# Forgetting attention with a GELU MLP on one core: the loads of batch 2's v issued by GpSimd, and two regroupings of matmuls

## The chip, the core and the metric

The kernel runs on one core of a Trainium2 chip. A core has a matrix engine (TensorE, "PE" in the profile; its weight loads are shown apart as "PEld"), a vector engine (VectorE, "DVE"), a scalar engine for activations (ScalarE, "ACT"), a general engine (GpSimd, "POOL") and an engine that mostly starts transfers (SyncE, "SP"). Transfers between main memory and the on-chip memory are moved by 16 DMA engines, whoever starts them. The engines run side by side, each through its own instructions in program order, and wait for one another by semaphores. Matmuls write to PSUM, a small memory of banks, from which VectorE or ScalarE must copy before a bank is used again.

The metric is the device time of one execution in microseconds (us).

## The reference

Eight batches of eight heads, 576 tokens, head width 64. Attention with a decay built from forget gates, causal, then a two-layer MLP with exact GELU over all 4608 tokens of width 512, inner width 2048:

```python
scores = scale * np.matmul(q, k.transpose(0, 1, 3, 2))
cum = np.cumsum(np.log(np.clip(f, 0.0001, 1.0)), axis=-1)
decay = cum[:, :, :, None] - cum[:, :, None, :]
scores = np.where(causal, -1000000000.0, scores + decay)
scores = scores - np.max(scores, axis=-1, keepdims=True)
attn = np.exp(scores)
attn = attn / (np.sum(attn, axis=-1, keepdims=True) + 1e-09)
x = np.matmul(attn, v)          # then (batch, token, head * 64)
...
h = x @ w_in
out = (0.5 * h * (1.0 + erf(h / sqrt(2)))) @ w_out
```

## The kernel before

**Stages of a batch.** The heads of a batch are worked in four pairs. For a pair, `scores` writes four tiles of scores (t = 0 to 3) to PSUM and ScalarE takes their exponentials (L312). Only what lies under the diagonal is computed, in the cuts of `STILES`. The diagonal blocks must be masked: for the pairs for which `on_pe` holds, PE adds a large negative number with further small matmuls (`after` and `key_of`) before the exponential; for all others GpSimd sets the masked places to zero afterwards (L314). `attend` (L333) multiplies the exponentials with the weighed v, `vw`, one head at a time, and `normalize` (L346, L347) divides by the sums, giving x. The decay is put into v: `weigh_v` (L271, GpSimd) multiplies v by weights per token. x is then transposed, by PE and a copy (`to_xT`, L366 and L369) in batches 0 and 1, by a transfer that SP starts (`x_dma`, L372) in the later ones. `gemm1` (L388) is the first GEMM: 16 blocks (`ffb`) of 128 inner columns, each of four matmuls, one per slice `kt` of 128 of the model width, that is, per head pair. After slice 3 ScalarE applies the Gelu (L408). Slice `kt` needs the transposed x of pair `kt`. The second GEMM of a batch is not a stage of its own: its matmuls are given out in steps, `take(fill, n)`, between the score and attention matmuls of the next batch, so that PE has work while ScalarE computes exponentials.

**The second GEMM of batch 0** is cut in three. `gemm2_first` (16 steps of one matmul, L520) runs in batch 1's attention with the first half of `w_out`, and its sums are kept in on-chip tiles `ot_of`, copied at L532. `gemm2_second` (L544) does the other half, the rows `kt` 8 to 15, in batch 2's attention: 8 steps into two banks of the pool `o`, then 8 steps into two banks of `m`. Each step is two matmuls of 64 rows. VectorE then adds both banks to `ot_of` (L552, then L504 in `sum_out`), which sets the banks free. `gemm2_rows` (L484) follows as the 17th step: by `PLAN_0` its first row of blocks takes the two `o` banks again.

**q and k.** GpSimd loads them a batch or more ahead (`load_qk_tokens`, L108). For batches from 2 on, SP transposes them by transfers (`transpose_dma`, L238: heads 0 to 3 of q, then of k, then heads 4 to 7 of each) into `tq` and `tk`, and VectorE sorts these into `qT` and `kT` (`untangle`, L252, eight copies for each pair). For batch 2 the `untangle` of its pairs 0 to 3 stands in VectorE's order beside the Gelu blocks 5, 8, 11 and 14 of batch 1, ahead of everything of batch 2's attention.

**v and w_out.** `load_v` loads v of a batch in five transfers (four of 256 KB and one of 128 KB), by SP unless told otherwise. There is a single buffer `v_sb`, free when the last `weigh_v` of the batch before is done. `w_out` comes in four quarters of 512 KB (`load_w_out`, L174, always GpSimd[...]); the quarters 2 and 3 hold the rows `kt` 8 to 11 and 12 to 15. They are issued in batch 1's attention after `behind` (L570), a small GpSimd copy that waits until k of batch 2 has landed.

**The order around the change.** It is written out by hand. In `second_attention` (batch 1), after the last scores, GpSimd has the gate and the two loads of `w_out`; SP has the four transposes of batch 2 (from 49.01 us) and, after the first blocks of the first GEMM, `load_v(2)`. GpSimd's next work after that are the copy of the tails (L378), `weigh_v(2, 0)` and `weigh_v(2, 1)`, then the loads of q and k of batch 3. In `attention` (batches 2 to 7) the first GEMM opens with five blocks whose slices are interleaved: the first two blocks in the two `m` banks, the next two in `o` banks (`spare()`), the fifth in a score tile (`more`). The other eleven follow one after the other.

Of the kernel before, what the change touches and what calls it, by code (L numbers as in the profile page):

```python
# [9 lines left out]
FP32 = mybir.dt.float32  # L10
# [5 lines left out]
P = 128  # L16
# [3 lines left out]
HP = 4  # L20
# [33 lines left out]
def kernel(  # L54
# [10 lines left out]
    nc = tc.nc  # L65
# [23 lines left out]
    s_psum = ctx.enter_context(tc.tile_pool(name="s_psum", bufs=2, space=PSUM))  # L89
# [25 lines left out]
    def load_v(b, h0=0, h1=H, eng=nc.sync, ns=range(NBLK)):  # L115
        if b >= B:
            return
        for n in ns:
            p0 = D if n == NBLK - 1 else 0
            eng.dma_start(  # L120
                v_sb[p0:P, h0:h1, n, :],
                v[b, h0:h1, K0[n] + p0 : K0[n] + P].rearrange("h p d -> p h d"),
            )
# [48 lines left out]
    def load_w_out(c):  # L172
        kt = slice(c * n_ff // 4, (c + 1) * n_ff // 4)
        nc.gpsimd.dma_start(w_out_sb[:, kt, :], w_out_r[:, kt, :])  # L174
# [105 lines left out]
    e_of = {}  # L280

    def scores(b, i, t):
        on_pe = b == 0 or (b == 1 and i == 0)
        st = s_psum.tile([P, 2, 512], FP32, tag="s", name=f"s{t}")
        c = 0
        for n, q0, w in STILES[t]:
            z = D if n == NBLK - 1 else 0
            masked = on_pe and c in SDIAG[t]
            for half in range(-1, 2 if masked else 0):
                if half == 0 and z:  # L290
                    continue
                for h in range(2):
                    d = slice(h * D, (h + 1) * D)
                    if half < 0:
                        to = st[:, h, c + z : c + w]
                        ab = kT[i][d, K0[n] : K0[n] + P], qT[i][d, q0 + z : q0 + w]
                    else:
                        last = (half + 1) * D
                        to = st[:, h, c + z : c + last]
                        c0 = (1 + h - half) * D  # L300
                        ab = key_of[d, c0 : c0 + P], after[d, c0 + z : c0 + last]
                    nc.tensor.matmul(  # L302
                        to, *ab, start=half < 0, stop=half == 1 or not masked
                    )
            c += w
        z = D if t == 1 else 0
        if z:
            et = e4[(b * HP + i) % len(e4)]
        else:
            et = e_pool.tile([P, 2, 512], BF16, tag=f"e{t}", name=f"e{t}")  # L310
        e_of[b, i, t] = et
        nc.scalar.activation(et[:, :, z:c], st[:, :, z:c], Act.Exp, scale=scale)  # L312
        for c0 in [] if on_pe else SDIAG[t]:
            nc.gpsimd.affine_select(  # L314
                out=et[:, :, c0 + z : c0 + P],
                in_=et[:, :, c0 + z : c0 + P],
                compare_op=Alu.is_ge,
                fill=0.0,
                base=z,
                pattern=[[0, 2], [1, P - z]],  # L320
                channel_multiplier=-1,
            )
# [31 lines left out]
    def xT(b):  # L354
        if b not in xT_of:
            xT_of[b] = xT_pool.tile([P, n_dm, XC], BF16, tag="xT", name="xT")
        return xT_of[b]
# [25 lines left out]
    def gemm1(c, ffb, kts=range(4), ps=None, act=True):  # L383
        src = xT(c) if c < B else tails
        if ps is None:
            ps = m_psum.tile([P, TC], FP32, tag="m", name="ps1")
        for kt in kts:
            nc.tensor.matmul(  # L388
                ps,
                w_in_sb[:, kt, ffb * P : (ffb + 1) * P],  # L390
                src[:, kt, 0:TC],
                start=(kt == 0),
                stop=(kt == n_dm - 1),
            )
        if n_dm - 1 in kts and act:
            gelu(c, ffb, ps)
        return ps

    def spare():
        return o_psum.tile([P, TC], FP32, tag="o", name="ps1")  # L400

    def gelu(c, ffb, ps):
        if c not in g_of:
            g_of[c] = [
                g_pool.tile([P, TC], BF16, tag=f"g{n}", name=f"g{n}")
                for n in range(n_ff)
            ]
        nc.scalar.activation(g_of[c][ffb], ps, Act.Gelu)  # L408
# [147 lines left out]
    def gemm2_third():  # L556
        yield from gemm2_second(0)
        yield from gemm2_rows(0, PLAN_0)
        yield from gemm2_rows(1, PLAN_1)

    def take(gen, n):
        for _ in range(n):
            if next(gen, "end") == "end":
                return


    def behind(t, h):

        g = x_pool.tile([P, 1], FP32, tag="gate", name="gate")
        nc.gpsimd.tensor_copy(g[:PT], t[:, h, 0:1])  # L570
# [109 lines left out]
    def attention(b):  # L680


        fill = gemm2_third() if b == 2 else gemm2_rows(b - 1, PLAN)
        counts = FILL_2 if b == 2 else FILL

        def av(i, n=0):
            for h in range(2):
                attend(b, i, h, (0, 1, 2, 3, 4))
                normalize(b, i, h)
                if h == 0:  # L690
                    take(fill, n)
            x_dma(b, i)

        for i in range(HP):
            for t in range(4):
                scores(b, i, t)
                take(fill, counts[i][t])
                if t == 1 and 0 < i < (HP if b == 2 else HP - 1):
                    av(i - 1)
                    if b == 2 and i == 1:  # L700
                        load_v(3)
                if b == 2 and (i, t) == (0, 3):
                    weigh_v(b, 2)
                    weigh_v(b, 3)
                if b > 2 and i == 0 and t == 1:
                    load_v(b + 1)
                if b > 2 and t == 0 and i < 2:
                    transpose_dma(b + 1, 4 * i, 4 * i + 4)
                if b == 2 and t == 1 and i == 1:
                    transpose_dma(3, 0, 4)  # L710
        if b == 2:
            take(fill, 4)
            av(HP - 1)
        else:
            av(HP - 2)
            take(fill, 3)
            av(HP - 1, 1)
            put_off.pop()()
        take(fill, 4)
        if b == 2:  # L720
            transpose_dma(3, 4, 8)
        take(fill, 999)

        pss = [gemm1(b, ffb, (0, 1)) for ffb in range(2)]
        for ffb in range(2):
            gemm1(b, ffb, (2,), pss[ffb])
        pss += [gemm1(b, ffb, (0, 1, 2), spare()) for ffb in (2, 3)]
        for ffb in range(4):
            gemm1(b, ffb, (3,), pss[ffb])
        more = s_psum.tile([P, 2, 512], FP32, tag="s", name="ps1")  # L730
        gemm1(b, 4, ps=more[:, 0, :])
        if b + 1 < B:
            untangle(b + 1, 0)
            weigh_v(b + 1, 0)
        x_tail(b)

    def second_attention():


        b, fill = 1, gemm2_first(0)  # L740

        def av(i, h):
            attend(b, i, h, (0, 1, 2, 3, 4))
            normalize(b, i, h)

        def transposes(i, pool, tag):
            for which in range(2):
                transposes_first(b, i, which, pool, tag)


        nc.scalar.activation(warm[0:1, 0:1], warm[0:1, 0:1], Act.Exp)
        def tiles(i, t):
            scores(b, i, t)
            scores(b, i, t + 1)

        def run(i):
            av(i, 0)
            av(i, 1)

        tiles(0, 0)  # L760
        transposes(1, o_psum, "o")
        transposes(2, m_psum, "m")
        transposes(3, o_psum, "o")
        tiles(0, 2)
        take(fill, 2)
        tiles(1, 0)
        run(0)
        tiles(1, 2)
        take(fill, 4)
        weigh_v(1, 2)  # L770
        tiles(2, 0)
        run(1)
        weigh_v(1, 3)
        tiles(2, 2)
        take(fill, 4)
        tiles(3, 0)
        transpose_dma(2, 0, 4)
        transpose_dma(2, 4, 8)
        to_xT(b, 0, nc.vector.tensor_copy, o_psum, "o")
        to_xT(b, 1, nc.vector.tensor_copy, o_psum, "o")  # L780
        take(fill, 2)
        tiles(3, 2)
        behind(qk_of[2][1], H - 1)
        load_w_out(2)
        load_w_out(3)
        run(2)
        take(fill, 4)
        av(3, 0)
        both = s_psum.tile([P, 2, 1024], BF16, tag="s", name="ps_x2")
        to_xT(b, 2, nc.scalar.copy, ps=both[:, 0, 0:XC])  # L790
        av(3, 1)
        gemm1_begin(1, both)
        x_tail(1)
        load_v(2)

    for b in range(B):
        if b == 0:
# [64 lines left out]
```

## Time and profile before

Five runs took 336.2 to 338.64 us, the median is 336.64. The profile is of one execution that took 336.2 us; its span, from the first to the last instruction, is 334.3 us.

| | us |
|---|---|
| median of five runs | 336.64 |
| profiled execution | 336.2 |
| its span | 334.3 |
| PE busy in 33 to 58 (batch 1's attention) | 22.99 of 25 |
| PE busy in 58 to 100 (batch 1's first GEMM, batch 2's attention) | 41.42 of 42 |
| PE busy in 100 to 288 | 185.57 of 188 |
| GpSimd stands before weighing v of batch 2 | 14.08 |

A row of the order by time reads: start, duration (both in us from the span's start), engine, line, operation, what it writes and what it reads, shapes, how many instructions were merged; in brackets the idle time of the engine before it and what ended it. An "issue" row on SP or POOL is the engine's time to start the transfer, not the transfer. The view of the transfers gives, for a stretch of time, each queue's packets, megabytes and the time that its packets took as a share of 16 engines; q0 is the queue of GpSimd's transfers, q1 that of SP's. Some matmul records are missing in a trace, so a count can be one or two short of what the program issues.

### The profile page before, as it was taken

How to read it: one execution, taken by the hardware profiler on the slowest of the kernel's cores; microseconds unless marked ns; L12 is line 12 of the kernel's file. 1: busy time of each engine (PE TensorE's matmuls, PEld its weight loads, DVE VectorE, ACT ScalarE, POOL GpSimd, SP SyncE). 2: the span in 40 equal slices, each digit the busy share in tenths (PEclk: the TensorE clock that was granted, in tenths of full speed). 3: DMA queues.
4: the chain of work that ended last, by engine and by line, in shares of the span. 5: the costliest groups of instructions: out<-in, count | busy, mean ns of one | idle time of the engine just before them, and what ended most of it. 6: DMA issues, size and time to landing. Idle time of an engine off the chain costs nothing.

```text
span 334.3 us, 7780 instructions
## 1 busy us (share of the span) xinstructions
PE 321.8 (96%) x3121; PEld 171.0 (51%) x3161; DVE 181.2 (54%) x420; ACT 206.6 (62%) x296; POOL 126.5 (38%) x252
## 2 busy tenths in 40 slices
PE   7899989999999999999999999999999999999995
PEld 3674556445554466445644565446544654444443
DVE  5770547664449845894589547954796550020011
ACT  3987797774635786478827892798278846404600
POOL 8880575047427054714444354525441420000000
PEclk9999999999999999999999999999999999999999
DMA  7999999969999799399938994869700241011013
GB/s 108 220 200 193 196 192 132 195 120 210 192 190 177 116 209 180 91 138 166 222 105 119 171 197 145 120 127 208 174 6 2 91 72 46 0 66 63 0 39 86
DMA packets 101747, 44.16 MB, mean 132 GB/s; under 512 B 80336, under 2 KB 96976, under 8 KB 101712
## 3 DMA queue, kind: packets, MB, share of 16 engines
q1 hardware_dynamic: 84112, 28.73, 43.7%
q0 software_dynamic: 17200, 14.42, 28.4%
q8 instruction: 24, 0.39, 0.5%
q10 hardware_dynamic: 400, 0.52, 0.4%
q14 instruction: 11, 0.09, 0.1%
HBM read 36.85 MB, written 9.44 MB: 138 GB/s over the span
## 4 chain that ended last, share of the span: by engine, by line
PE 90%; issue 2%; DMA 2%; POOL 2%; DVE 1%; ACT 1%; POOLq 0%; ACTq 0%; DVEq 0%
PE ps L388 36%; PE ps L484 26%; PE o L333 10%; PE ps L424 8%; PE s L302 7%; DMA v_sb<-in_v_dram 2%; PE ps L544 1%; PE ps_x L366 1%; ACT e L312 1%; POOL q L108 1%; POOL k L108 1%; DVE qT L219 0%; DVE kT L219 0%; PE ps L520 0%; PE ps_f L208 0%
## 5 line engine op out<-in xcount | busy, mean ns | idle before, releaser
L408 ACT ACTIVATE g<-ps 128x512 bf16<-128x512 f32 x144 | 82.1, 601 | 83.8 <-PE ps L388 83.8
L312 ACT ACTIVATE e<-s 128x896 bf16<-128x896 f32 (+2 forms) x128 | 100.0, 836 | 21.1 <-PE s L302 18.4
L388 PE MATMUL ps<-xT,w_in_sb 128*128 128x512 bf16 x497 | 111.8, 379 | 0.7
L484 PE MATMUL ps<-w_out_sb,g 64*128 64x512 bf16 (+1 forms) x692 | 104.4, 376 | 1.6 <-issue 1.3
L388 PEld LDWEIGHTS <-w_in_sb 128*128 128x128 bf16 x576 | 55.9, 98 | 67.8 <-issue 2.3
L314 POOL TENSOR_SCALAR_AFFINE_SELECT e<-e 128x256 bf16<-128x256 bf16 (+1 forms) x135 | 49.3, 386 | 89.4 <-ACT e L312 89.1
L484 PEld LDWEIGHTS <-g 64*128 64x128 bf16 (+1 forms) x711 | 39.4, 95 | 34.8 <-issue 4.2
L271 POOL TENSOR_TENSOR vw<-v_sb,wT 128x640 bf16<-128x640 f32 x30 | 38.6, 1289 | 27.1 <-PE ps L544 14.1
L302 PE MATMUL s<-qT,kT 64*128 64x320 bf16 (+4 forms) x384 | 43.4, 276 | 2.9 <-ACT e L312 2.1
L252 DVE COPY kT<-tk 64x288 bf16<-64x288 bf16 x96 | 41.9, 436 | 3.6 <-DMA tk<-k 2.0
L252 DVE COPY qT<-tq 64x288 bf16<-64x288 bf16 x96 | 40.8, 425 | 1.7 <-DMA tq<-q 0.3
L492 DVE COPY ot<-ps 128x512 f32<-128x512 f32 x20 | 13.8, 692 | 47.0 <-PE ps L484 47.0
L333 PEld LDWEIGHTS <-e 128*128 128x128 bf16 x960 | 34.5, 98 | 8.1 <-POOL e L314 2.5
L333 PE MATMUL o<-vw,e 128*128 128x65 bf16 x960 | 37.2, 194 | 0.9 <-issue 0.8
L347 DVE TENSOR_TENSOR x<-o,r 128x320 bf16<-128x320 f32 x64 | 31.4, 491 | 2.7 <-DMA xT<-x 0.6
L433 DVE COPY ot<-ps 128x512 f32<-128x512 f32 (+2 forms) x9 | 5.7, 632 | 49.7 <-PE ps L424 49.7
L302 PEld LDWEIGHTS <-kT 64*128 64x128 bf16 x384 | 19.7, 94 | 23.8 <-issue 6.9
L424 PE MATMUL ps<-w_out_sb,g 128*128 128x512 bf16 (+2 forms) x142 | 27.9, 355 | 0.1
L424 PEld LDWEIGHTS <-g 128*128 128x128 bf16 x144 | 13.5, 98 | 14.5
L346 DVE RECIPROCAL r<-o 128x5 f32<-128x5 f32 x64 | 12.0, 188 | 11.2 <-PE o L333 11.1
L504 DVE TENSOR_TENSOR ot<-ot,ps 128x512 f32<-128x512 f32 x22 | 15.1, 685 | 1.1
L388 PE MATMUL ps<-tails,w_in_sb 128*128 128x512 bf16 x63 | 14.2, 377 | 0.1
(68 smaller groups left out, 137.9 us busy)
## 6 DMA issues: line engine op xcount, KB each, us to landing
out_dram<-ot SPq DMA_DIRECT2D x32, 256.0 KB, 2.5
v_sb<-in_v_dram SPq DMA_DIRECT2D x24, 256.0 KB, 4.6
q<-in_q_dram POOLq DMA_DIRECT2D x6, 576.0 KB, 6.3
k<-in_k_dram POOLq DMA_DIRECT2D x6, 576.0 KB, 8.4
v_sb<-in_v_dram SPq DMA_DIRECT2D x17, 128.0 KB, 4.9
w_in_sb<-in_moe_w_in_dram POOLq DMA_DIRECT2D x4, 512.0 KB, 8.2
w_out_sb<-in_moe_w_out_dram POOLq DMA_DIRECT2D x4, 512.0 KB, 9.4
v_sb<-in_v_dram POOLq DMA_DIRECT2D x5, 128.0 KB, 6.0
```

The lines of the kernel that those rows point to most:

```text
L252: nc.vector.tensor_copy(rows[:, odd], src[odd * D : (odd + 1) * D, 2 * i + h].rearrange("d j p -> d p j"),)
L271: eng.tensor_tensor(vw(b)[:, hs, n0:n1, 0:D], v_sb[:, hs, n0:n1, :], w.unsqueeze(3).to_broadcast([P, 2, n1 - n0, D]), Alu.mult,)
L302: nc.tensor.matmul(to, *ab, start=half < 0, stop=half == 1 or not masked)
L312: nc.scalar.activation(et[:, :, z:c], st[:, :, z:c], Act.Exp, scale=scale)
L314: nc.gpsimd.affine_select(out=et[:, :, c0 + z : c0 + P], in_=et[:, :, c0 + z : c0 + P], compare_op=Alu.is_ge, fill=0.0, base=z, pattern=[[ ...
L333: nc.tensor.matmul(o[:, m, :], e_of[b, i, t][:, h, c : c + P], vw_of[b][:, 2 * i + h, n, :], start=(n == 0), stop=(n == m),)
L347: nc.vector.tensor_tensor(x_of[b, i][:, :, h, :], o[:, :, 0:D], r.unsqueeze(2).to_broadcast([P, NBLK, D]), Alu.mult,)
L388: nc.tensor.matmul(ps, w_in_sb[:, kt, ffb * P : (ffb + 1) * P], src[:, kt, 0:TC], start=(kt == 0), stop=(kt == n_dm - 1),)
L408: nc.scalar.activation(g_of[c][ffb], ps, Act.Gelu)
L424: nc.tensor.matmul(pss[ts][:, c0:c1], g_of[c][kt][:, ts * P : (ts + 1) * P], w_out_sb[:, kt, c0:c1], start=(kt == 0), stop=(kt == n_ff - 1),)
L484: nc.tensor.matmul(banks[r], g_of[c][kt][rows, ts * P : (ts + 1) * P], w_out_sb[rows, kt, :], start=kt == (steps.index("r") if r else 0), ...
L504: nc.vector.tensor_tensor(ot, ot, bank, Alu.add)
```

## The change

It has four edits.

1. The mask of pair 3's tile 3 in batch 1 is done by PE instead of GpSimd.
2. Two steps of `gemm2_first` are taken earlier: four instead of two after pair 0's scores, two instead of four before `av(3, 0)`. The number in all stays 16.
3. `load_v(2)` is issued by GpSimd, between the gate and the two last quarters of `w_out`, instead of by SP at the end of `second_attention`.
4. In `attention` the opening of the first GEMM takes slices 0 and 1 of four blocks, then their slice 2, then slices 0 to 2 of the fifth block, then slice 3 of all five. Before, slice 2 of the first two blocks came after four matmuls and the fifth block followed whole.

```diff
     def scores(b, i, t):
-        on_pe = b == 0 or (b == 1 and i == 0)
+        on_pe = b == 0 or (b == 1 and (i == 0 or (i, t) == (HP - 1, 3)))
...
         pss = [gemm1(b, ffb, (0, 1)) for ffb in range(2)]
-        for ffb in range(2):
+        pss += [gemm1(b, ffb, (0, 1), spare()) for ffb in (2, 3)]
+        for ffb in range(4):
             gemm1(b, ffb, (2,), pss[ffb])
-        pss += [gemm1(b, ffb, (0, 1, 2), spare()) for ffb in (2, 3)]
-        for ffb in range(4):
+        more = s_psum.tile([P, 2, 512], FP32, tag="s", name="ps1")
+        pss.append(gemm1(b, 4, (0, 1, 2), more[:, 0, :]))
+        for ffb in range(5):
             gemm1(b, ffb, (3,), pss[ffb])
-        more = s_psum.tile([P, 2, 512], FP32, tag="s", name="ps1")
-        gemm1(b, 4, ps=more[:, 0, :])
...
         tiles(0, 2)
-        take(fill, 2)
+        take(fill, 4)
         tiles(1, 0)
...
         behind(qk_of[2][1], H - 1)
+        load_v(2, eng=nc.gpsimd)
         load_w_out(2)
         load_w_out(3)
         run(2)
-        take(fill, 4)
+        take(fill, 2)
         av(3, 0)
...
         gemm1_begin(1, both)
         x_tail(1)
-        load_v(2)
```

## The prediction

> **What bounds the kernel now.** I read the page's busy shares first, then the chain of waits. The profiled execution took 336.2 us, its span is 334.3; the median of the runs, 336.64, is 0.44 above it.
>
> ```profile
> span 334.3 us, 7780 instructions
> ...
> PE 321.8 (96%) x3121; PEld 171.0 (51%) x3161; DVE 181.2 (54%) x420; ACT 206.6 (62%) x296; POOL 126.5 (38%) x252
> ```
>
> Both say TensorE; "POOL 38%" says nothing of when GpSimd's work is due. So a gain can only be a hole in PE that closes, and a loss is whatever makes PE stand. Busy time by stretch (33 to 58, 58 to 100, 100 to 288 us) gives PE 22.99 of 25.00, 41.42 of 42.00 and 185.57 of 188.00 us: what can be won is about 2 us in batch 1's attention, which the order by time shows to be rounds between PE and ScalarE:
>
> ```profile
> 42.30 0.37 PE L302 MATMUL s<-qT,kT 64*128 64x256 bf16 x4 [0.41 <-ACT e L312]
> 42.89 0.34 PE L302 MATMUL s<-qT,kT 64*128 64x64 bf16 x4 [0.23 <-ACT e L312]
> ```
>
> PE waits there until an exp has freed one of two score tiles.
>
> **Part 1, batch 1's attention.** Two steps of `gemm2_first` move ahead to 41.50, where two steps of 0.216 us stand before the 0.41 us hole. Four end at 41.50 + 0.86 = 42.36; with 0.10 for the change from whole-array matmuls to scores (a GEMM of 64 x 0.216 = 13.81 us takes 13.91 to the next score) the scores of pair 1 start at 42.46 instead of 42.30. Those 0.16 us pass through the exps and shrink, as every round has a 0.23 us hole; I carry 0.05 to the scores (3,3) at 51.22. These now take the mask on PE: masked scores took 41.17 to 41.50, unmasked ones 51.22 to 51.45, so +0.09. Pair 2's attention thus ends 0.14 later. Then two steps fewer (-0.43), and the mask that GpSimd had at 53.07 (408 ns) no longer holds `attend(3, 0)`, whose sixth matmul stood 0.10. PE would be 0.39 ahead, but the transposes of pair 2 (L366, 53.86) wait for VectorE's x, which comes 0.14 later, at 53.62: they start at 53.67. **Gain 0.19 us**. The ot copy of the moved steps comes earlier and nobody waits for it.
>
> **Part 2, the opening of the first GEMM in batches 2 to 7.** It moves slice 2 from position 4 to 8 and slice 3 from 12 to 15. From the first matmul to the next stage the six GEMMs take 13.91, 13.91, 14.01, 13.91, 13.91 and 13.95 us (the last without the 0.10): only two hold a stall, 0.10 and 0.14, because the transposed x landed late. Gain 0.24. Its price: block 5 reuses block 0's bank five matmuls (1.08 us) after block 0's last. The first Gelu starts 0.41 after that matmul (137.89 to 138.31) and takes 0.60, so 1.01: hidden, by 0.07; were that cover gone, 0.05 a batch. **Gain 0.2 us**.
>
> **Part 3, v of batch 2.** Removed from SP: five issues of 10.15 us in all, for which nobody waits (SP's next work is a store at 72.59). The loads end in the 14 us for which GpSimd stands before weighing:
>
> ```profile
> 53.54 1.57 POOL L174 DMA_DIRECT2D w_out_sb<-in_moe_w_out_dram  x2
> 55.02 2.37 SPq L238 DMA_TRANSPOSE tk<-k  x1
> 57.49 10.15 SPq L120 DMA_DIRECT2D v_sb<-in_v_dram  x5
> 71.20 1.28 POOL L271 TENSOR_TENSOR vw<-v_sb,wT 128x640 bf16<-128x640 f32 x1 [14.08 <-PE ps L544]
> ```
>
> (L544 is not what it waits for; the last v packet moves at 70.2.) That wait costs nothing today: vw of batch 2 is first read at 80.33. So removing it brings 0. What counts is what the loads now stand before. On GpSimd five issues of 0.63 to 0.79 us (its own rows for v at 8 to 13 us), 3.6 us, go ahead of the two w_out loads, from about 53.0 to 56.7; behind them also stands the copy of batch 1's tails (56.71), which nobody reads before 302 us. And in the transfers: today v lies on SP's queue *behind* the transposes of batch 2's q and k; now it lies *beside* them. VectorE waits for those already:
>
> ```profile
> 62.37 1.34 DVE L252 COPY qT<-tq 64x288 bf16<-64x288 bf16 x4 [0.27 <-DMA tq<-q]
> 65.75 1.35 DVE L252 COPY kT<-tk 64x288 bf16<-64x288 bf16 x4 [2.04 <-DMA tk<-k]
> 67.11 1.34 DVE L252 COPY qT<-tq 64x288 bf16<-64x288 bf16 x4
> 68.46 1.34 DVE L252 COPY kT<-tk 64x288 bf16<-64x288 bf16 x4
> 71.16 0.69 DVE L552 TENSOR_TENSOR ot<-ot,ps 128x512 f32<-128x512 f32 x1 [1.36 <-PE ps L544]
> 71.88 0.69 DVE L504 TENSOR_TENSOR ot<-ot,ps 128x512 f32<-128x512 f32 x1
> ```
>
> Behind the copy that waits for tk stand two more copies (2.7 us) and the two adds that free the o banks. PE's 17th filling step (`PLAN_0`, L484, 73.03) takes those banks. So PE starts that step at (start of the kT copy) + 4.05 + 1.41 + 0.05 = start + 5.51. Today that is 71.26 and PE comes at 73.03: the last transpose may be 1.77 us later than 65.75, and no more.
>
> How late will it be? The DMA view of three stretches, 57 to 63, 9 to 12 and 13 to 15 us (packets, MB, share of 16 engines):
>
> ```profile
> q0 software_dynamic: 921, 0.93, 91.6%
> q1 hardware_dynamic: 927, 0.23, 30.4%
> ...
> q0 software_dynamic: 452, 0.33, 72.2%
> q1 hardware_dynamic: 1252, 0.31, 53.2%
> ...
> q0 software_dynamic: 168, 0.45, 104.6%
> ```
>
> q0 is GpSimd's queue, q1 SP's. In the first, w_out (1 KB packets) and the transposes (256 B) share the engines packet for packet. In the second v on SP beside GpSimd's q and k had 2.8 packets for one. The third is v on GpSimd alone: 109 of its 168 packets are of 4 KB, 55 a us, 290 ns each on its engine. No row shows that beside transposes; its cost is bounded by these shares.
>
> Two rules of the Trainium skill's page "DMA: Bandwidth & Descriptors" are to be weighed. Its section "Issuing engines are not separate DMA queues" says that the issuer changes only the issue time, since all transfers run on the same engines. By it part 3 costs 0 and the sum is 336.2 - 0.4 = 335.8. The section "Queues, rings and completion order" says that an engine takes turns between its queues a whole packet at a time. By it a 256 B transpose packet waits for a 4 KB one each time, which speaks against the change. The row 57 to 63 agrees with the second, the row 9 to 12 doesn't; I work out both.
>
> *One for one.* Transposes still to move when v starts (first packet 1.7 after the issue, as w_out: 54.7): two of 1152 packets, 2304. First 1.6 us as slow as w_out's start (55.2 to 56.8: 251 packets of q1), to 56.3. Then v, 1.18 MB = 288 packets at 51 a us (290 ns and 25 for a transpose packet): 5.6 us, to 61.9, with 288 transposes. Then w_out, 1024 at 150 a us (921 in 6): 6.8 us, to 68.7, with 1024. Left: 2304 - 251 - 288 - 1024 = 741. Meanwhile v has landed (62.9), GpSimd weighs (3.0) and issues q and k of batch 3 at 66 instead of 73.95, so q0 never runs dry; beside such loads q1 moved 972 packets in 29 to 34 us, 194 a us: 3.8 us, to 72.5. VectorE started 1.0 after the last packet (64.7, 65.75): 73.5. PE's step: 79.0 instead of 73.03, **+6.0 us**, whatever part 1 won before, as the transfers set it.
>
> *Three for one beside v, one for one beside w_out.* v 288 at 44 a us: 6.5 us with 864 transposes, to 62.8; w_out to 69.6 with 1024; left 165, 0.9 us: copy at 71.5, step at 77.0, **+4.0**.
>
> I take the first, as the row with the same transposes on the same queues is the nearest. Sum: 336.2 + 6.0 - 0.2 (part 2) = 342.0, or **342.5** on the median. With the lower share 340.5; with slower starts or copies slowed by GpSimd's work (600 ns instead of 330 each at 136 us, so up to +3.2) 345.5.
>
> **Rivals.** *w_out late.* If the transposes keep three for one throughout, 1189 are left after v at 62.8; a round of one w_out packet (95 ns) and three of 25 takes 171 ns, so 281 a us: done at 67.0, copy at 68.0, and VectorE costs 0.5. But 630 packets of w_out are left then: 3.8 us, landed at 71.8. Its last quarter is needed at 69.23 + 4 x 0.216 = 70.1: PE stands 1.7 us in L544, together 338.1 on the median (336.64 + 1.7 - 0.2, rounded). For it: the row 9 to 12; against it: 57 to 63.
>
> *The loads are hidden; not slower.* GpSimd's transfer is the more compact (16 times fewer packets for the same bytes), all ends by 69, as the bytes are the same and the first of them start 0.5 us earlier. Then parts 1 and 2 remain: 336.2. It holds as long as the last transpose lands before 67.5. Against it: v ended at 70.2 with the same bytes, and now the transposes get the small share of a mix that lasts as long.
>
> *A real gain.* Over 1.7 us would need most of the holes of batch 1, of which the edit fills one; its best sum is 0.39 + 0.24.
>
> **Chances.** VectorE's stall 0.67, w_out late 0.13, hidden 0.15, a gain 0.05. About 0.5% (1.7 us) is what this kernel's measurement tells from no change. Slower: the first two, 0.80; same 0.15; faster 0.05. The range 337 to 345.5 leaves out the last two but for a little, and 0.02 at the top.
>
> **What would show it.** Right: the kT copies from tk start after 70 us with a long DMA wait; idle time of PE before a L484 step near 73 with VectorE's add (L504) as releaser; GpSimd's weighing at 63. Wrong: kT copies as today; PE idle at 69 to 71 in L544 (w_out); or the scores of batch 2 start later than 69.0, which would put the loss in part 1.

## The result and the profile after

| | before | after |
|---|---|---|
| median, us (runs) | 336.63 (48) | 339.93 (27) |
| lowest to highest, us | 335.88 to 339.89 | 336.61 to 344.71 |
| ratio of the times, 95% interval | | 1.0064 [1.0045, 1.0083] |
| profiled execution, us | 336.2 | 340.52 |
| its span, us | 334.3 | 338.6 |

The change makes the kernel slower, by 0.64%, which is 2.15 us (336.63 x 0.0064; 1.5 to 2.8 by the interval). The forecast was 5.9 us slower (342.5 against 336.64). The ratios, here and below, leave out executions more than 1.5% above a kernel's fastest (here eight, at 342.1 to 344.7 us, seven of them at a granted clock of 0.99), which the medians keep; the traces below show that a long stand of PE costs clock, so the true harm is rather above 0.64% than below. The lowest time lies within the range of before and the highest is 5 us above it: something in the changed kernel is decided anew in each execution.

The line of busy shares in the page of the changed kernel says little by itself: PE is busy for 2.6 us more in a span that is 4.3 longer.

```profile
PE 324.4 (96%) x3125; PEld 172.4 (51%) x3165; DVE 184.0 (54%) x420; ACT 205.8 (61%) x296; POOL 131.1 (39%) x256
```

So I cut the traces at points that both kernels have: the first scores of batch 1, the first scores of batch 2, the opening of batch 2's first GEMM, the end. All lengths are in us, from the order by time.

| kernel | batch 1's scores to batch 2's | batch 2's scores to its GEMM | its GEMM to the end |
|---|---|---|---|
| before | 31.25 | 31.45 | 233.79 |
| after | 31.12 | 33.66 | 233.68 |
| after, profiled again (e8) | 31.12 | 33.42 | 233.64 |

The first and the third stretch are shorter than before (the small gains of parts 1 and 2), the second is 2.0 to 2.2 longer. (The first profile of the changed kernel also came 2.3 us late to batch 1's scores, 40.11 instead of 37.78. Up to there the two programs are the same. Two other traces, e4 without v on GpSimd and e6 with it, are 1.0 us late at this point. The cause was not looked for, and I leave the delay out; the times of the first profile below are to be read 2.2 us earlier.)

What happens in the second stretch? First PE in the order by time, before and then after:

```profile
69.23 1.89 PE L544 MATMUL ps<-w_out_sb,g 64*128 64x512 bf16 x16
71.12 1.89 PE L544 MATMUL ps<-w_out_sb,g 64*128 64x512 bf16 x16
73.03 1.89 PE L484 MATMUL ps<-w_out_sb,g 64*128 64x512 bf16 x16
```

```profile
71.43 1.03 PE L544 MATMUL ps<-w_out_sb,g 64*128 64x512 bf16 x8
73.31 1.04 PE L544 MATMUL ps<-w_out_sb,g 64*128 64x512 bf16 x8 [0.85 <-DMA w_out_sb<-in_moe_w_out_dram]
...
76.73 0.37 PE L484 MATMUL ps<-w_out_sb,g 64*128 64x512 bf16 x1 [0.30 <-DVE ot L552]
77.45 1.88 PE L484 MATMUL ps<-w_out_sb,g 64*128 64x512 bf16 x15 [0.35 <-DVE ot L504]
```

There are two new waits. After four steps of `gemm2_second`, PE stands for the last quarter of `w_out` (0.85 us); and the 17th step, L484, waits for both of VectorE's adds, as the forecast had it, but for 0.30 and 0.35 us instead of six. Counted from batch 2's first scores, the last L544 comes 1.03 us later than before and the second L484 another 1.18: in the order of time, 1.0 us passes at `w_out` and 1.2 at VectorE. VectorE's rows and GpSimd's of the same trace show where the second comes from:

```profile
69.13 3.44 DVE L252 COPY kT<-tk 64x288 bf16<-64x288 bf16 x4 [2.77 <-DMA tk<-k]
72.58 1.77 DVE L252 COPY qT<-tq 64x288 bf16<-64x288 bf16 x4
74.36 1.60 DVE L252 COPY kT<-tk 64x288 bf16<-64x288 bf16 x4
75.99 0.69 DVE L552 TENSOR_TENSOR ot<-ot,ps 128x512 f32<-128x512 f32 x1
76.71 0.69 DVE L504 TENSOR_TENSOR ot<-ot,ps 128x512 f32<-128x512 f32 x1
```

```profile
55.32 4.27 POOL L120 DMA_DIRECT2D v_sb<-in_v_dram  x5
...
69.25 1.33 POOL L271 TENSOR_TENSOR vw<-v_sb,wT 128x640 bf16<-128x640 f32 x1 [7.51 <-DMA v_sb<-in_v_dram]
```

The kT copies, which waited for tk until 65.75 before, start at 66.9 on the clock of before (69.13 less 2.2), not at 73.5 as forecast. They then take 3.44 + 1.77 + 1.60 = 6.81 us for twelve instead of 4.03, while GpSimd weighs v beside them from 69.25 on. And v is there at 67.0 (69.25 less 2.2), not at 62.9. Both terms of the forecast are off, in opposite directions.

The two waits of PE are not parts of a sum. The first add (75.99) follows the copies without a pause, so it did not wait for PE. The copies start 1.2 us later than before and take 2.8 us longer; less the slack of 1.77, that is 2.2 us, the whole by which the stretch grew. With `w_out` in time PE would have stood as long, all of it at L484. The wait for `w_out` lies inside VectorE's delay. (This is worked out from the trace; no run took the wait for `w_out` away and left the copies late.)

### The profile page after: what moved, and what is told of

Its sections match the earlier page's. It is cut to its first block, busy times and chain, and to the rows that moved or that the text cites. A ratio compares the mean times of both kernels' runs of the same rounds, so it can differ in the third digit from the quotient of the medians.

```text
span 338.6 us, 7790 instructions
## 1 busy us (share of the span) xinstructions
PE 324.4 (96%) x3125; PEld 172.4 (51%) x3165; DVE 184.0 (54%) x420; ACT 205.8 (61%) x296; POOL 131.1 (39%) x256
## 4 chain that ended last, share of the span: by engine, by line
PE 75%; DMA 15%; POOL 3%; DVE 2%; issue 2%; SPq 1%; ACT 0%; POOLq 0%; ACTq 0%
PE ps L388 28%; PE ps L484 26%; PE ps L424 8%; PE o L333 7%; DMA v_sb<-in_v_dram 6%; PE s L302 5%; DMA tk<-k 3%; DMA k<-in_k_dram 3%; DMA w_in_sb<-in_moe_w_in_dram 3%; DVE kT L252 1%; SPq L238 1%; POOL q L108 1%; POOL vw L271 1%; POOL k L108 1%; DVE qT L252 1%
## 5 line engine op out<-in xcount | busy, mean ns | idle before, releaser
L408 ACT ACTIVATE g<-ps 128x512 bf16<-128x512 f32 x144 | 81.0, 603 | 84.7 <-PE ps L388 84.7
L484 PE MATMUL ps<-w_out_sb,g 64*128 64x512 bf16 (+1 forms) x692 | 104.8, 376 | 2.2 <-issue 1.3
L484 PEld LDWEIGHTS <-g 64*128 64x128 bf16 (+1 forms) x711 | 40.3, 95 | 35.5 <-issue 5.4
L252 DVE COPY kT<-tk 64x288 bf16<-64x288 bf16 x96 | 44.6, 464 | 4.3 <-DMA tk<-k 2.8
L302 PE MATMUL s<-qT,kT 64*128 64x320 bf16 (+4 forms) x384 | 44.4, 276 | 1.9 <-ACT e L312 1.0
L504 DVE TENSOR_TENSOR ot<-ot,ps 128x512 f32<-128x512 f32 x22 | 15.1, 685 | 1.1
```

Source lines behind the costliest of these rows:

```text
L252: nc.vector.tensor_copy(rows[:, odd], src[odd * D : (odd + 1) * D, 2 * i + h].rearrange("d j p -> d p j"),)
L302: nc.tensor.matmul(to, *ab, start=half < 0, stop=half == 1 or not masked)
L484: nc.tensor.matmul(banks[r], g_of[c][kt][rows, ts * P : (ts + 1) * P], w_out_sb[rows, kt, :], start=kt == (steps.index("r") if r else 0), ...
L504: nc.vector.tensor_tensor(ot, ot, bank, Alu.add)
```

## Experiments

### Which part carries the loss: e1, e2 and e4

e1 is the kernel before with the move of v alone, e2 the changed kernel with v given back to SP at its old place, e4 the new opening alone.

```diff
         behind(qk_of[2][1], H - 1)
+        load_v(2, eng=nc.gpsimd)      # e1: on the kernel before
         load_w_out(2)
...
         x_tail(1)
-        load_v(2)                     # e1
```

> Part 3 alone: the kernel before, with load_v(2) issued by GpSimd ahead of the last quarters of w_out. Theory A (the transfers): w_out's last quarter and the transposes of k land late, PE stands about 0.9 us at the first L544 steps and up to 1 us at the first L484 step near 73 us; 1.5 to 3.5 us slower than before, as the whole change. Theory B (the loss lies in part 1 or 2, in the mask on PE, the moved steps or the five Gelus in a row): no change, within 0.5 us. Theory C (my forecast, transposes one packet for one of v): 4 to 6 us slower, with the copy from tk starting after 71 us.

> Parts 1 and 2 without part 3: the changed kernel with load_v(2) given back to SP at the end of second_attention. Theory A: 0.2 to 0.4 us faster than before (the sum of my parts 1 and 2), no stall in L544 or in the first L484 step. Theory B: about 2 us slower than before.

> Part 2 alone: the kernel before with only the new opening of the first GEMM in batches 2 to 7. Theory A and my forecast: 0 to 0.25 us faster, the stalls of 0.10 and 0.14 us in two of the six openings gone. Theory B (five Gelus in a row hold block 5 back): each opening longer by 0.1 to 0.4 us, 0.6 to 2.4 us slower in all.

| | median, us | ratio to before |
|---|---|---|
| e1, part 3 alone | 339.23 | 1.004 [1.0019, 1.006] |
| e2, parts 1 and 2 | 336.52 | 1.0001 [0.9984, 1.0018] |
| e4, part 2 alone | 336.4 | 0.9998 [0.9981, 1.0015] |

Part 3 carries the loss. The other two are too small for the times, but the traces show them: the stretch from batch 1's scores to batch 2's is 31.24 in e1 and 31.25 in e4, which lack part 1, and 31.12 in e2, which has it. In e2's trace batch 2's attention takes 31.45 as before: no wait is left.

The profiled execution of e1 took 343.37 us, 4.1 above its median. In it PE stands 3.5 us for `w_out` in one piece and 0.3 in another, no add of VectorE is waited for, and the stretch is 6.7 longer. But VectorE is late there too:

```profile
73.12 1.34 DVE L252 COPY kT<-tk 64x288 bf16<-64x288 bf16 x4 [7.50 <-DMA tk<-k]
```

This is 0.4 us from the 73.5 of the forecast, and 5.5 us of lateness for L484 by its chain; PE does not wait for the adds only because `w_out` and the lower clock hold it longer (L484 starts at 79.84). The same two delays stand side by side, both larger than in the changed kernel's traces. How often an execution goes this way is not known: the longest ones of the changed kernel have no trace.

### Before or behind w_out: e3

Is it enough that `w_out` goes first? In e3 GpSimd issues v after the two quarters.

```diff
-        load_v(2, eng=nc.gpsimd)
         load_w_out(2)
         load_w_out(3)
+        load_v(2, eng=nc.gpsimd)
```

> The changed kernel with GpSimd's load_v(2) behind the two quarters of w_out instead of ahead of them. Theory A with the order on GpSimd's queue as the cause: w_out lands at about 64 us again, L544 does not stand; if the 4 KB packets of v leave the transposes their share (as the trace of the changed kernel suggests, with 300 to 570 transpose packets a us beside them) k's transposes land by 66 and the time is 0 to 0.4 us below before. Theory C (one packet for one): from 63 us on the transposes get 51 packets a us while v takes 5.6 us, the copy from tk starts at about 70 us and the kernel is 2 to 3 us slower than before.

The median is 346.09, ratio 1.0285 [1.0261, 1.031], the worst kernel of all, and 9.6 us slower where one packet for one had been expected to cost 2 to 3. PE and VectorE by time:

```profile
79.77 4.29 PE L484 MATMUL ps<-w_out_sb,g 64*128 64x512 bf16 x16 [6.68 <-DVE ot L552]
```

```profile
69.69 1.34 DVE L252 COPY qT<-tq 64x288 bf16<-64x288 bf16 x4 [6.97 <-DMA tq<-q]
72.24 3.00 DVE L252 COPY kT<-tk 64x288 bf16<-64x288 bf16 x4 [1.21 <-DMA tk<-k]
75.26 2.38 DVE L252 COPY qT<-tq 64x288 bf16<-64x288 bf16 x4
77.66 1.33 DVE L252 COPY kT<-tk 64x288 bf16<-64x288 bf16 x4
79.03 0.69 DVE L552 TENSOR_TENSOR ot<-ot,ps 128x512 f32<-128x512 f32 x1
```

Read them from the bottom: the add that PE waits for comes straight after the copies, the copies straight after the transfer of tk. This is the forecast's chain in full and alone, since `w_out` is in time: late transposes, late and slow copies, late adds, and PE standing 6.68 us at the step that was named. It is what the forecast expected of the other order. The transfers between 64 and 68 us show its share, packet for packet:

```profile
q0 software_dynamic: 257, 0.84, 95.5%
q1 hardware_dynamic: 256, 0.06, 11.0%
```

While v's 4 KB packets (0.84 MB in 257) move on GpSimd's queue, SP's queue gets one 256 B packet for each, 64 a us.

### Are late copies the link? e5 and e6

In both, the last two `untangle` of batch 2 are moved behind adds in VectorE's order (after scores (0, 2) and (1, 0) of batch 2), where late transposes can't hold the adds up: e5 on e3, e6 on the changed kernel.

```diff
+                if b == 2 and (i, t) in ((0, 2), (1, 0)):
+                    untangle(b, 2 + i)
...
-                if late == 0:
+                if late == 0 and (b > 1 or at < 2):
                     untangle(b + 1, at)
```

> As e3_v_behind (9.5 us slower than before, PE 7.0 us at the first L484 step), but VectorE sorts q and k of pairs 2 and 3 of batch 2 later: untangle(2, 2) after the scores (0, 2) and untangle(2, 3) after the scores (1, 0) of batch 2, behind the adds that free the o banks. Theory A2 (the late transposes reach PE only through VectorE's order): the stall goes, time 0 to 0.5 us below before, though k's transposes land as late as in e3_v_behind, near 72 us. Theory B2 (PE stands for the transfers themselves, or for vw or w_out): still more than 3 us slower than before.

> The changed kernel with the same later place of untangle(2, 2) and untangle(2, 3). What is left is w_out behind v on GpSimd's queue. Theory A2: the L484 step does not stand, but L544 still does, 0.5 to 3.5 us, so 0.5 to 3.5 us slower than before (up to the whole loss of the change). If w_out were never late and only VectorE's order counted: within 0.4 us of before.

e5: 344.11, ratio 1.0216 [1.0198, 1.0235]. e6: 343.52, ratio 1.0135 [1.0099, 1.0171]. In e5 the step at 73 us no longer waits; its last L544 and first L484 come as early as before. So the order on VectorE was the link in e3. But the cure costs nearly as much as it saves. VectorE and GpSimd in e5:

```profile
74.63 6.11 DVE L252 COPY qT<-tq 64x288 bf16<-64x288 bf16 x4
80.75 1.55 DVE L252 COPY kT<-tk 64x288 bf16<-64x288 bf16 x4
82.33 0.69 DVE L492 COPY ot<-ps 128x512 f32<-128x512 f32 x1
```

```profile
75.91 1.84 POOL L314 TENSOR_SCALAR_AFFINE_SELECT e<-e 128x256 bf16<-128x256 bf16 x5
77.72 1.27 POOL L271 TENSOR_TENSOR vw<-v_sb,wT 128x640 bf16<-128x640 f32 x1
79.11 1.27 POOL L271 TENSOR_TENSOR vw<-v_sb,wT 128x640 bf16<-128x640 f32 x1
```

Four copies take 6.11 us instead of 1.34, one of them 3593 ns, while GpSimd works with hardly a pause; then PE waits 2.12 and 2.45 us for VectorE further on. My expectation had left this collision out. In e6, PE's wait for `w_out` is still there (1.49 idle, the last L544 1.94 late), which no order on VectorE could remove, and the same collision adds a wait of 2.45 for VectorE at 87.21. So in the changed kernel the wait for `w_out` is a second thing beside VectorE, not its consequence, and about as long: taking VectorE's lateness away at this place left 1.94 us.

### The size of the load, and the change once more: e7 and e8

e7 lets GpSimd load the heads 0 to 3 ahead of `w_out` and SP the heads 4 to 7 at the old place. e8 is the changed kernel itself.

```diff
-        load_v(2, eng=nc.gpsimd)
+        load_v(2, 0, 4, nc.gpsimd)
...
         x_tail(1)
+        load_v(2, 4, 8)
```

> The changed kernel with only heads 0 to 3 of v issued by GpSimd ahead of w_out (0.59 MB instead of 1.18), heads 4 to 7 by SP at the end of second_attention as before. If the loss goes with the bytes ahead of w_out, w_out lands about 3 us earlier than in the changed kernel: L544 does not stand; the transposes of k lie beside 144 instead of 288 packets of v; loss of 0 to 1 us. If what counts is that GpSimd's queue holds v packets of 4 KB at all, about the loss of the changed kernel, 2 us.

> The changed kernel once more, beside the others. 1.5 to 3 us slower than before, with a wide spread of its runs; a second trace, to see whether L544 and the first L484 step stand in it again and by how much: 0.5 to 4 us and 0 to 1 us. The 2.2 us that its first trace lost before 36 us should not come again.

e7: 336.96, ratio 1.0004 [0.9987, 1.0022]; the stretch is 31.46, no wait is left, though the kT copy starts at 66.59, 0.84 later than before (the eight copies ahead of it took 5.21 us instead of 2.68 while GpSimd weighed v and issued loads): within the slack of 1.77. e8: 339.46, ratio 1.0123 [1.0078, 1.0167] from six executions, 4.1 us by the ratio where 1.5 to 3 had been expected. Its PE and VectorE:

```profile
71.76 1.04 PE L544 MATMUL ps<-w_out_sb,g 64*128 64x512 bf16 x8 [1.35 <-DMA w_out_sb<-in_moe_w_out_dram]
```

```profile
69.22 1.34 DVE L252 COPY kT<-tk 64x288 bf16<-64x288 bf16 x4 [4.62 <-DMA tk<-k]
70.57 1.34 DVE L252 COPY qT<-tq 64x288 bf16<-64x288 bf16 x4
71.92 1.55 DVE L252 COPY kT<-tk 64x288 bf16<-64x288 bf16 x4
73.50 0.69 DVE L552 TENSOR_TENSOR ot<-ot,ps 128x512 f32<-128x512 f32 x1
```

In the order of time 1.72 of the 1.97 us pass at `w_out` (the last L544 against before) and 0.25 at VectorE. But here too the add follows the copies without a pause. The copies start 3.5 us later than before and take 0.2 longer; less 1.77, that is the whole 2.0 us again. In both profiles of this kernel VectorE's chain ends last and the wait for `w_out` lies inside its delay. The transfers of e8 from 57.2 to 63.1 us, while v moved (packets, MB, share of 16 engines), show where the forecast's arithmetic broke:

```profile
q0 software_dynamic: 341, 1.13, 83.8%
q1 hardware_dynamic: 1210, 0.30, 27.9%
```

The transposes put through 1210 packets beside v's 288 of 4 KB, where the forecast had 251 in v's slow start and 288 beside it, 539 in all. In the first profile of the change they put through even 2262 (57.2 to 66 us). The queues don't go side by side but by turns of a us or two: from 59 to 61 us of e8 the two queues moved 79 and 1153. Only after v, beside `w_out`, do they go packet for packet: 449 and 444 from 65 to 68 us, and 449 in 3 us are the 150 a us that the forecast had put in.

### Why v's queue pauses, and v held back: e9 and e10

One guess for the pauses was that VectorE's copies hinder GpSimd in issuing v. In e9 a small copy of Gelu block 3 keeps VectorE from the copies until 59.8. In e10 GpSimd issues v only behind `w_out` and a gate on tk's last transfer.

```diff
+                if b == 1 and ffb == 5:                    # e9
+                    hold = x_pool.tile([P, 1], FP32, tag="hold", name="hold")
+                    nc.vector.tensor_copy(hold, g_of[1][3][:, 0:1])
```

```diff
-        load_v(2, eng=nc.gpsimd)                           # e10
         load_w_out(2)
         load_w_out(3)
+        g = x_pool.tile([P, 1], FP32, tag="gate", name="gate")
+        nc.gpsimd.tensor_copy(g[:PT], tq_of[2][1][:PT, H - 1, JT // 2 - 1, 0:1])
+        load_v(2, eng=nc.gpsimd)
```

> The changed kernel, but VectorE's copies of q and k of batch 2 (untangle) begin only after the Gelu of block 3, at about 59.8 us, when GpSimd has issued all its loads. In the traces of the changed kernel GpSimd's queue runs dry for 1 to 2 us after v's first transfer while VectorE copies, and in that time the transposes of q pass alone. Theory D (VectorE's copies hold back GpSimd's writing of transfers): v's five issues take about 0.75 us each instead of 0.9, v moves without a pause at about 50 packets a us and has landed by 63.5, w_out's last quarter lands about 1 to 2 us earlier, and the transposes share one packet for one, so that k's land after 71 us. PE then stands at the first L484 step for 3 us or more, as I forecast, and the time is 3 to 8 us above before. Rival: the pause has another cause; then v moves with the same pause and q's transposes pass in it at 500 or more packets a us.

> The changed kernel with GpSimd's load_v(2) behind the two quarters of w_out and behind a small GpSimd copy that waits until k's last transpose has landed, so that v lies beside no transpose. If the loss comes from v lying beside the transposes and ahead of w_out: no stall at L544 nor at the first L484 step, v landed at about 72 to 73 us as in the kernel before, 0 to 0.4 us below before. If v on GpSimd's queue costs by itself (issue time, VectorE, its landing): more than 0.5 us above before.

The guess falls. e9 took 342.06, ratio 1.0153 [1.013, 1.0177]; GpSimd's issues took as long as in e8 (0.70 to 0.95 us each). VectorE stood idle from 56.7 to 59.8, and within that time, from 57 to 58 us, v's queue had a pause all the same:

```profile
59.81 0.15 DVE L824 CAST hold<-g 128x1 f32<-128x1 bf16 x1 [3.15 <-ACT g L408]
...
q1 hardware_dynamic: 477, 0.12, 98.7%
q0 software_dynamic: 4, 0.01, 3.5%
```

PE stands for `w_out` twice in it, 2.01 and 1.50 us. Why v's queue lets the transposes pass is left open.

e10 took 337.95, ratio 1.0047 [1.0025, 1.0069]. No matmul waits for `w_out` any more, and its stretch is 0.97 longer, not 2.0. What is left is GpSimd's issuing beside VectorE's copies, which its order by time shows:

```profile
66.39 1.94 DVE L252 COPY kT<-tk 64x288 bf16<-64x288 bf16 x4
68.35 2.17 DVE L252 COPY qT<-tq 64x288 bf16<-64x288 bf16 x4
```

GpSimd issues v from 66.35 to 70.93. Four copies take 1.94 and 2.17 us instead of 1.34, and the second L484 starts 0.32 late. The rest, 0.65, passes in the first attention matmuls of batch 2, where PE waits for a mask (0.21 idle at 81.64): GpSimd comes to the masks later, as it weighs v from 75.87. I had expected it to be no slower than before, and was wrong. Its trace also has two slow openings of the first GEMM (15.55 and 14.2 us instead of 13.91) where a transposed x landed late; whether v's place causes these I did not test (e1 and e2 each have one opening of 14.2 and 14.13). No version that puts all of v on GpSimd's queue was as fast as before, and none of the ten kernels was measurably faster than it.

## Why the prediction was wrong, step by step

- **What bounds the kernel.** Right: TensorE, and the loss is PE standing in batch 2's attention, where the slack was counted. It is the only stretch that grew. Both signs that the forecast had named came in the first profile: PE idle before L484 with L504 as the releaser (right), and PE idle in L544 for `w_out` (wrong).
- **Part 1, gain 0.19.** Right in sign, a little smaller: 31.25 to 31.12, 0.13 us.
- **Part 2, gain 0.2.** Right in the openings, and too small for the times. The six openings are 13.91 but for the last, 13.81; 14.01 and 13.95 have become 13.91 and 13.81. The stretch that holds them is shorter by 0.11 (after) and 0.15 (e8). No Gelu stall came: the cover of 0.07 held.
- **The wait of 14.08 us costs nothing.** Right: v is usable earlier than the 71.20 of before (67.0 in after, 64.54 in e8) and nothing is gained by it.
- **One for one, with v at 51 packets a us from 56.3 on.** This is the step that failed: a term of the sum, not the chain. It took the share of the row 57 to 63 us for a stretch in which v's queue came in bursts with pauses. The issues took 4.28 us, not 3.6, and v's first packet moved at 57.2 in e8, not at 54.7; what the transposes had left then was nearly as forecast (2366 packets from 57.2 to 68.7 us in e8, 2304 forecast). But 1210 of them moved beside v in e8 and 2262 in after, not 539. So the copies that wait for the last of them started 3.5 us later than before in e8 (69.22) and 1.2 in after, not 7.75 (73.5). After the slack of 1.77, and with copies slower by 0.2 and 2.8 us, which the forecast had only in its upper limit, VectorE's chain is late by 2.0 and 2.2 us, where 6.0 was forecast. That is the whole lengthening.
- **`w_out` beside it.** v was usable at 64.54 in e8, not 62.9, and `w_out` at 71.76, not 69.7. It holds PE up by 1.7 (e8) and 1.0 us (after), within the time that VectorE takes anyway.
- **The rivals.** "w_out late" named a wait that came. It gave 68.0 for the copies and 71.8 for `w_out`; e8 has 69.22 and 71.76, the last in part by luck, since after has 71.1 and the profiled e1 75.2. Its time, 338.1, lies 0.7 below the measured 338.8 (336.63 x 1.0064). It had VectorE cost 0.5, hidden behind `w_out`; the traces have VectorE at 2.0 to 2.2, not hidden. And its reason, three packets for one *throughout*, is wrong: beside v the transposes had 4 (e8) to 8 (after) for each of v's 288 packets, beside `w_out` 444 to 449. "Hidden" and "gain" fall with e1 and e2.
- **The two rules weighed.** The Trainium skill's page "DMA: Bandwidth & Descriptors", "Issuing engines are not separate DMA queues", had been read as making part 3 free: e1 with its 1.004 [1.0019, 1.006] says no, as what counted was not the issue time but which transfers stood beside and behind which. Turns of whole packets, which "Queues, rings and completion order" states for queues that an engine has work for, agree with e3 (257 to 256). The 1153 to 79 of e8 do not look like such turns; whether v's queue had work then, no run shows.
- **The mechanism that was forecast exists.** It ends last in both traces of the change, and e3, with v *behind* `w_out`, shows it alone, at 6.68 us. Ahead of `w_out`, it is smaller, because the transposes pass during v's pauses.

The range, 337 to 345.5, held the time, but not for the forecast's reason: the sums of its two shares were 342.5 and 340.5, and only its lower end, below the rival at 338.1, took in 338.8. The row 9 to 12 us, with 2.8 packets for one, was v beside a loaded queue as well; I had called it the further one because its queues were exchanged, and even it was too low.

## What to carry to other kernels

When a load changes queues, work out what lands later for every transfer beside it and behind it, and which consumer of those has the least slack; the load's own consumer may be the one that doesn't matter. A share between two queues read in one stretch (921 to 927 here) need not hold in another, where one queue pauses (79 to 1153): bound that case by the rows with the most uneven shares, and let both cases into the sum, since they shift lateness from one neighbour to another. When two waits follow each other on the engine that bounds the kernel, ask whether the second would have been as long without the first, before counting them as a sum. And where there is slack, the size counts as well as the place: half of the load (e7) cost nothing, all of it 2 us in the same place and 9.6 behind `w_out`.

## What the runs showed of the hardware

**A long stand costs twice.** Two stretches of e3, the stand and what follows (columns: stretch, length, busy time of PE, PEld, DVE, ACT and POOL with instructions, granted clock, DMA share, GB/s):

```profile
73.00:79.00 6.00, 0.09 (x2) 0.00 (x0) 5.86 (x11) 0.92 (x1) 4.46 (x8) 0.73 0.61 75
80.00:83.00 3.00, 2.86 (x14) 1.01 (x13) 1.72 (x3) 0.00 (x0) 0.00 (x0) 0.50 1.29 231
```

When PE comes back the granted clock is 0.50, and matmuls follow one another after 427 ns instead of 216 for some 6 us. Of the 10.25 us that e3's stretch is longer, the stand itself is about 7. One stand of 3.5 us (e1) and two of 2.01 and 1.50 within 4.5 us (e9) lost clock too, down to 0.50. Length alone doesn't decide below that: stands of 0.85 (after), 1.35 (e8), 1.49 and 2.45 us (e6) lost none, but in e5 one of 2.12 us did:

```profile
83.20:84.30 1.10, 1.01 (x30) 0.92 (x28) 1.09 (x3) 0.00 (x0) 0.00 (x0) 1.00 0.19 29
84.40:84.90 0.50, 0.50 (x3) 0.08 (x3) 0.49 (x2) 0.00 (x0) 0.00 (x0) 0.50 0.63 221
```

There PE had stood until 83.07, and the next stand, 2.45 us, began only after these rows. The Trainium skill's page "TensorE: Matmul & The Clock Gate", "Part 1: The HAM clock gate", names an idle window of about 3.4 us for the fall to half rate. The stands of e1 and e3 are that long, but these traces agree only in part: the mean of 0.73 in e3's first row, taken as a stretch at 1.00 and then one at 0.50, puts the fall some 2.7 us into the stand (an estimate from that row), and e5 fell after a stand of 2.12. For a forecast it means that a stand of 3.5 us or more is to be priced with about 3 us on top (e1: 3.8 of 6.7; e3: 7 of 10.25), and one of 2 us or more may be.

**VectorE's copies can starve beside GpSimd.** A copy of 64x288 bf16 takes 0.33 us alone (four in 1.34) and took up to 3593 ns in e5 beside GpSimd's work with hardly a gap. The Trainium skill's page "SBUF — State Buffer", "SBUF: two separate sides", says that the two engines share a port pair as an exclusive lock for the length of an instruction. The longest GpSimd instruction there took 1.28 us, so one lock alone doesn't explain 3.6; that the copy lost the port several times in a row fits, but was not tested.
